# An experts' loop with branches: one region of fixed order instead of many, and the next expert's rows requested ahead of the branch

## The chip, the cores and the metric

The kernel runs on one core of one Trainium2 chip. The metric is device time in microseconds (us) for one execution; lower is better. Engines are named as the profile names them: PE is TensorE (matmul), PEld its weight loads, DVE is VectorE, ACT is ScalarE, POOL is GpSimd, SP is SyncE, which here only issues DMA transfers. A name with a q behind it (PEldq, SPq) is an engine's instruction sequencer.

## What is computed

Three layers run one after the other: clustered attention, a dense feed-forward layer with a softmax gate, and a mixture of eight experts. The change touches the third alone:

```python
logits = x @ w_gate                       # x: 1536 tokens of 512
expert_idx = np.argmax(logits, axis=1)    # one of 8 experts per token
...
h = np.maximum(np.einsum('ecd,edf->ecf', disp, w1), 0.0)   # 512 -> 1024
y = np.einsum('ecf,efd->ecd', h, w2)                       # 1024 -> 512
...
out[i] = gate_w[i] * y[expert_idx[i], pos[i]]
```

Each expert takes at most 384 tokens. How many it gets is known only when the chip has computed the gate, so the kernel branches on the counts.

## The kernel before

Attention and the dense layer are planned together by a small list scheduler (class Plan), whose emit writes all instructions in a fixed order; the gate then counts the tokens of each expert (tile cnt) and scatters the token rows, sorted by expert, to a DRAM tensor xs. From there the experts' part begins (method run of class Experts). This is its vocabulary:

- rows (L1030) asks for an expert's token rows by one transposing DMA on SP into the tile cxT; idf (L1034) asks for the tokens' numbers; ids (L1039) is the DVE cast of these to integers. xload (L1043) puts the three into a plan. The tiles come from a pool of two, so the rows of expert e+1 take the place of those of expert e-1, and the request waits until PE has finished with these.
- gemm1 (L1059) is the first product of an expert for one slice of 128 hidden units: 12 matmuls on a 16-bit high and low part of weights and rows (ah, al and the two halves of cxT). evac (L1072) clears a PSUM bank: ACT writes the high half of the hidden layer (hr, L1076), DVE the low half (L1077).
- gemm2 (L1079) is the second product: 24 matmuls of 512 columns for 128 tokens into one bank. scale (L1086) moves it to the tile yo on ACT, put (L1089) scatters yo to the output by an indirect DMA of POOL.
- A weight piece (c_weights, L970) is a DMA of 512 KB on SP (L988), then ACT makes the 16-bit high part (L991) and DVE the low part (L992). There are eight per expert. Block e asks for expert e+2's pieces 2 to 7 and expert e+3's pieces 0 and 1, into a ring of eight buffers, and block e+1 converts them; the converts wait in the list later/last for that.

The order of the work: extra(-1) handles expert 0's first 128 tokens, first its second 128 (L1196 comes between the two and stands for eight register loads of the counts, one per expert). Then, for e = 1 to 7, block(e) runs rows2 inside one of two branches, with 256 tokens if the count r is over 192, else with 192; rows2 does gemm1 for the eight slices in four banks and converts three weight pieces between. After the branch, second does 2 x 24 gemm2 matmuls, five more pieces are converted and the next eight are asked for. Behind each expert stands a second branch (L1203), taken when it has more than 256 tokens: extra(e, 2, 2) does the third 128.

What sets the order: inside a region opened by manual_schedule the instructions keep the order in which they were written. Between regions the tile framework's scheduler is free. In the kernel before, each branch's body, first and the part behind each branch are regions of their own, and the If blocks themselves and the loop around them stand outside any; so the scheduler has moved instructions and whole branches against each other. On PE, the branch of expert e+1 (L1146) now stands ahead of the branch L1203 of expert e and, from e = 1 on, ahead of part of the gemm2 matmuls of expert e.

A branch L1203 that is not taken has an else side in which each engine waits for its own last instruction and adds what the body would have added to its semaphore. Without this the counts of the semaphores would differ between the two ways.

Of the kernel before, what the change touches and what calls it, by code (L numbers as in the profile page):

```python
# [21 lines left out]
NT = B * S  # L22
DM = H * D
DF = 1024
E = 8
CAP = 384
P = 128
# [13 lines left out]
HALF = 64  # L41
# [150 lines left out]
def ring(pool, name, n, shape, dt):  # L192
    return [pool.tile(shape, dt, tag=f"{name}{i}", name=f"{name}{i}") for i in range(n)]
# [497 lines left out]
class Moe1:  # L691
# [262 lines left out]
    def run(self, order, t):  # L954
        self.t = t
        for kind, i in order:
            getattr(self, kind)(i)
# [12 lines left out]
def c_weights(tc, pools, w1, w2):  # L970
    nc = tc.nc
    W = {}

    def piece(e, i, run=lambda eng, f: f()):
        src, kh, kl, n = ((w1, "ah", "al", KC), (w2, "bh", "bl", FC))[i // 4]
        g = i % 4
        m = n // 4
        gs = slice(g * m, (g + 1) * m)
        box = []

        def load():
            if i == 0:
                W[e] = {k: pools["cw"].tile([P, c, d], F16, tag=k, name=f"{k}_{e}")
                        for k, c, d in (("ah", KC, DF), ("al", KC, DF), ("bh", FC, DM), ("bl", FC, DM))}
            late = 8 * e + i >= FIRST
            t = pools["cs2" if late else "cst"].tile([P, m, DF * DM // (n * P)], F32, tag="wst", name=f"w_{e}_{i}", bufs=LATE if late else 3)
            box.append(t)
            nc.sync.dma_start(out=t, in_=src[e, g * m * P : (g + 1) * m * P].rearrange("(c p) f -> p c f", p=P))  # L988

        run("sp", load)  # L990
        run("act", lambda: nc.scalar.activation(W[e][kh][:, gs], box[0], AF.Copy, scale=64.0))  # L991
        run("dve", lambda: nc.vector.scalar_tensor_tensor(out=W[e][kl][:, gs], in0=box[0], scalar=64.0,  # L992
                                                          in1=W[e][kh][:, gs], op0=ALU.mult, op1=ALU.subtract))

    return W, piece


def c_piece(nc, plan, piece, e, i, at, later=None):

    n = 8 * e + i  # L1000
    j = n % 3 if n < FIRST else 3 + (n - FIRST) % LATE
    cost = dict(sp=0.6, act=0.95, dve=1.14)

    def run(eng, f):
        if eng == "sp":
            plan.add(eng, cost[eng], at, f, reads=["turn"], writes=[("cst", j)], data=0.52)
        elif later is None:
            plan.add(eng, cost[eng], at + 6, f, reads=[("cst", j)], writes=[("cw", e, i)])
        else:
            later.append((f, lambda at: plan.add(eng, cost[eng], at, f, reads=[("cst", j)], writes=[("cw", e, i)])))  # L1010

    piece(e, i, run)


class Experts:
# [125 lines left out]
    def block(self, e, start, r):  # L1141
        plan = self.plan
        plan.banks = [(0.0, k) for k in self.two]
        self.hidden(e, 2)
        last, self.later = self.later, []
        with self.tc.If(r > P + HALF) as c:  # L1146
            with self.tc.manual_schedule():
                self.rows2(e, 2 * P, last[:6])
        with c.Else():
            with self.tc.manual_schedule():  # L1150
                self.rows2(e, P + HALF, last[:6])
        with self.tc.manual_schedule():
            if e + 1 < E:
                self.xload(e + 1, 0.0, [(0, CAP)], (4.0,))
            for n, (_, conv) in enumerate(last[6:]):
                conv(1.2 + 1.2 * (n // 2))
            for n, i in enumerate(range(8 * e + start, min(8 * e + start + 8, 8 * E))):
                c_piece(self.nc, plan, self.piece, i // 8, i % 8, 0.5 + 1.0 * n, self.later)
            self.second(e, 0, 2, 0.0, [], CAP)
            plan.emit()  # L1160
# [13 lines left out]
    def run(self, ctx, start, cnt, cnt0):  # L1174
        tc, nc, plan = self.tc, self.nc, self.plan
        self.xk = ctx.enter_context(tc.tile_pool(name="cx", bufs=2))
        self.pools["cs2"] = ctx.enter_context(tc.tile_pool(name="cs2", bufs=LATE))
        one = ctx.enter_context(tc.tile_pool(name="c1", bufs=1))
        self.yo = ring(one, "yo", 3, [P, DM], F32)
        self.hr = [ring(one, f"hr{i}", 2, [P, FC, 2 * P], F16) for i in range(2)]  # L1180
        for h in self.hr:
            for x in h:
                nc.vector.memset(x[:, :, P + HALF :], 0.0)
        self.bank = [plan.banks.pop(0)[1] for _ in range(2)]
        self.four, self.two = [k for _, k in plan.banks[:4]], [k for _, k in plan.banks[4:]]
        plan.MIX, plan.WIN, plan.lean, plan.marks = 0.1, 0.05, {}, ()
        r0 = nc.values_load(cnt0[0:1, 0:1], min_val=0, max_val=NT)
        self.hidden(-1, 1)
        with tc.If(r0 > P - 1) as full:
            self.extra(-1, 0, 2)  # L1190
        with full.Else():
            self.rows(-1, 0, P)
            self.idf(-1, 0, P)
            self.ids(-1, 0, P)
            self.extra(-1, 0, 2)
        regs = [nc.values_load(cnt[0:1, i : i + 1], min_val=0, max_val=NT) for i in range(E)]  # L1196
        for e in range(E):
            if e:
                self.block(e, start, regs[e])
            else:  # L1200
                with tc.manual_schedule():
                    self.first(start)
            with tc.If(regs[e] > 2 * P):  # L1203
                self.hidden(e, 1)
                self.extra(e, 2, 2)


@with_exitstack
# [153 lines left out]
```

## Time and profile before

| | us |
|---|---|
| three runs | 573.86, 576.17, 578.21; median 576.17 |
| the profiled execution | 570.86 |
| span of its trace | 569.1 (1.8 lies around it) |
| PE busy | 495.2 (87%) |
| DVE, ACT, POOL busy | 414.0, 365.0, 277.4 |
| granted TensorE clock, mean | 0.966 of full speed |

Times in the trace count from the span's start. The experts' part runs from 383 to the end. PE's busy time counts overlapping matmuls once, and a matmul's end is modelled, so the distance between the starts of two matmuls tells more than the length of one. The experts differ: the trace has 256-column matmuls for experts 2 and 3, 192 columns for 1 and 4 to 7, and one taken branch L1203, that of expert 2.

### The profile page before, as it was taken

The numbers are of one execution on the slowest core, as the hardware profiler recorded it, in microseconds if no ns is written. First come the engines' busy times: TensorE is split into PE (matmuls) and PEld (weight loads), VectorE is DVE, ScalarE is ACT, GpSimd is POOL, SyncE is SP. The second block draws the span as 40 slices with busy tenths as digits, with TensorE's granted clock in tenths as the row PEclk, the third lists the DMA queues.
The fourth block names the chain that finished last, engine by engine and source line by source line (L and its number), as shares of the span: only waits on it lengthen the run. The fifth ranks groups of instructions, "written<-read, shape, count | busy, mean of one in ns | idle before, by whom it ended". The sixth has DMA issues, their size and how long they took to land. (4 is left out here: it accounts for less than half of the span.)

```text
span 569.1 us, 13148 instructions
## 1 busy us (share of the span) xinstructions
PE 495.2 (87%) x4945; PEld 323.1 (57%) x4945; DVE 414.0 (73%) x980; ACT 365.0 (64%) x553; POOL 277.4 (49%) x292
## 2 busy tenths in 40 slices
PE   1578899889688988989989989989799999999796
PEld 1356676666465554645544444447567585677462
DVE  6699979999989799998655999981276254756310
ACT  3576778988867888978754999941256253755220
POOL 2256788999969868898762245431000201010011
PEclk9987989999979999999999999999989999999899
DMA  8898858796769799999999788974956757889400
GB/s 246 251 183 222 251 161 224 221 278 161 174 173 214 169 239 152 196 229 168 240 186 195 214 232 203 221 191 119 313 163 245 209 192 217 241 305 294 71 20 22
DMA packets 159347, 113.85 MB, mean 200 GB/s; under 512 B 126560, under 2 KB 135074, under 8 KB 159268
## 3 DMA queue, kind: packets, MB, share of 16 engines
q1 hardware_dynamic: 156660, 106.31, 75.9%
q0 software_dynamic: 2320, 6.32, 3.1%
q8 instruction: 51, 0.84, 0.6%
q14 instruction: 28, 0.23, 0.1%
q10 hardware_dynamic: 288, 0.16, 0.1%
HBM read 51.57 MB, written 17.11 MB: 121 GB/s over the span
## 5 line engine op out<-in xcount | busy, mean ns | idle before, releaser
L409 POOL TENSOR_TENSOR pr<-pf,pr 128x384 f16<-128x384 f32 x168 | 173.7, 1064 | 53.2 <-ACT pr L461 24.8
L1090 POOL DMA_INDIRECT out_dram<-yo,ids x16 | 16.0, 1000 | 154.2 <-ACT yo L1087 130.1
L1063 PE MATMUL psb<-cxT,ah 128*128 128x192 f16 (+2 forms) x288 | 69.9, 254 | 8.7 <-DMA cxT<-xs 5.2
L503 DVE TENSOR_REDUCE mm<-psb 128x1 f32<-128x384 f32 x132 | 66.9, 546 | 6.7 <-PE psb L500 6.5
L1064 PE MATMUL psb<-cxT,ah 128*128 128x192 f16 (+2 forms) x288 | 69.8, 254 | 0.0
L1065 PE MATMUL psb<-cxT,al 128*128 128x192 f16 (+2 forms) x288 | 69.8, 254 | 0.0
L537 PE MATMUL psS<-QK 96*128 96x384 f32 x132 | 62.4, 507 | 0.0
L500 PE MATMUL psb<-QK 96*128 96x384 f32 x132 | 47.9, 422 | 15.4 <-DVE mm L503 11.2
L545 ACT ACTIVATE pf<-psS 128x768 f32<-128x768 f32 x66 | 53.0, 803 | 8.4 <-PE psS L537 7.0
L545 ACT ACTIVATE pr<-psS 128x768 f16<-128x768 f32 x66 | 52.6, 803 | 7.8 <-PE psS L537 7.3
L992 DVE SCALAR_TENSOR_TENSOR bl<-w,bh 128x1024 f16<-128x1024 f32 x32 | 39.0, 1229 | 20.4 <-ACT bh L991 19.8
L536 PE MATMUL psS<-QK 128*128 128x384 f16 x132 | 46.9, 355 | 1.7 <-ACT pr L545 1.0
L558 PE MATMUL psb<-V,pr 128*128 128x65 f16 x396 | 43.5, 196 | 3.9 <-DVE mm L503 3.1
L992 DVE SCALAR_TENSOR_TENSOR al<-w,ah 128x1024 f16<-128x1024 f32 x32 | 40.5, 1279 | 7.9 <-ACT ah L991 7.8
L1076 ACT ACTIVATE hr<-psb 128x384 f16<-128x384 f32 (+1 forms) x28 | 14.6, 520 | 47.3 <-PE psb L1065 47.3
L1083 PE MATMUL psb<-bl,hr 128*128 128x512 f16 x112 | 42.5, 379 | 0.9 <-PEq L1203 0.6
L560 PE MATMUL psb<-V,pr 128*128 128x65 f16 x396 | 43.1, 194 | 0.1
L559 PE MATMUL psb<-V,pr 128*128 128x64 f16 x396 | 43.2, 197 | 0.0
L1077 DVE SCALAR_TENSOR_TENSOR hr<-psb,hr 128x384 f16<-128x384 f32 (+1 forms) x28 | 16.6, 593 | 36.3 <-ACT hr L1076 36.3
L1082 PE MATMUL psb<-bh,hr 128*128 128x512 f16 x112 | 42.4, 379 | 0.3
L1084 PE MATMUL psb<-bh,hr 128*128 128x512 f16 x112 | 42.4, 379 | 0.1
L558 PEld LDWEIGHTS <-pr 128*128 128x128 f16 x396 | 37.2, 98 | 7.4 <-issue 2.5
(202 smaller groups left out, 1576.5 us busy)
## 6 DMA issues: line engine op xcount, KB each, us to landing
w<-in_w_dram SPq DMA_DIRECT2D x64, 512.0 KB
xs<-X SPq DMA_DIRECT2D x12, 516.0 KB
QK<-hr SPq DMA_DIRECT2D x16, 384.0 KB
QK<-hl SPq DMA_DIRECT2D x32, 192.0 KB
x<-in_qkT_dram SPq DMA_DIRECT2D x7, 768.0 KB
lT<-in_w_in_dram SPq DMA_DIRECT2D x8, 512.0 KB
lT<-in_w_out_dram SPq DMA_DIRECT2D x8, 512.0 KB
v<-in_vP_dram SPq DMA_DIRECT2D x8, 384.0 KB
```

The lines of the kernel that those rows point to most:

```text
L409: nc.gpsimd.tensor_tensor(out=out[:, i], in0=a[:, i], in1=b[:, i], op=ALU.subtract)
L500: add("pe", 0.18, at(c - 10 + 0.25 * g), lambda c=c, g=g, w=w: nc.tensor.matmul(w.bank[:, :384], q1[:, c * P : (c + 1) * P], k1[:, g * 384 ...
L503: add("dve", 0.465, at(c - 9.9 + 0.25 * g), lambda c=c, g=g, w=w: nc.vector.tensor_reduce(out=m2[mm][:, c, g : g + 1], in_=w.bank[:, :384] ...
L536: nc.tensor.matmul(o, k2[:, ks], q2[:, qs], start=True, stop=False)
L537: nc.tensor.matmul(o, k1[:, ks], q1[:, qs], start=False, stop=True)
L545: add("act", 0.691, at(k + 0.5), lambda dst=dst, kb=kb: nc.scalar.activation(dst, ps[kb][:, :, :384], AF.Exp, scale=SC), reads=[kb], write ...
L558: nc.tensor.matmul(A, ph[ub][:, c, qs], v[:, j, c, 0:65], start=(c == 0), stop=False)
L559: nc.tensor.matmul(A[:, :64], ph[ub][:, c, qs], v[:, j, c, 65:129], start=False, stop=False)
L992: run("dve", lambda: nc.vector.scalar_tensor_tensor(out=W[e][kl][:, gs], in0=box[0], scalar=64.0, in1=W[e][kh][:, gs], op0=ALU.mult, op1=A ...
L1063: nc.tensor.matmul(o, w["ah"][:, c, fs], x[:, 0, c, a:b], start=(c == 0), stop=False)
L1064: nc.tensor.matmul(o, w["ah"][:, c, fs], x[:, 1, c, a:b], start=False, stop=False)
L1065: nc.tensor.matmul(o, w["al"][:, c, fs], x[:, 0, c, a:b], start=False, stop=(c == KC - 1))
```

## The change

The loop over the experts, with the register loads, stands in one manual_schedule region, the If blocks included; the regions inside the two branches are gone. So every engine gets its instructions, branches too, as the program writes them. All eight counts are loaded into registers at the top. The rows and numbers of expert e+1 are asked for ahead of the two branches of expert e, not in the plan behind them; the cast ids stays in the plan.

```diff
         last, self.later = self.later, []
+        if e + 1 < E:
+            self.X[e + 1] = self.tiles(self.xk, e + 1, CAP)
+            self.rows(e + 1, 0, CAP)
+            self.idf(e + 1, 0, CAP)
         with self.tc.If(r > P + HALF) as c:
-            with self.tc.manual_schedule():
-                self.rows2(e, 2 * P, last[:6])
+            self.rows2(e, 2 * P, last[:6])
         with c.Else():
-            with self.tc.manual_schedule():
-                self.rows2(e, P + HALF, last[:6])
+            self.rows2(e, P + HALF, last[:6])
         with self.tc.manual_schedule():
             if e + 1 < E:
-                self.xload(e + 1, 0.0, [(0, CAP)], (4.0,))
+                plan.add("dve", 0.07, 9.0, lambda: self.ids(e + 1, 0, CAP), writes=[("ids", ((e + 1) % 2, CAP))])
...
-        regs = [nc.values_load(cnt[0:1, i : i + 1], min_val=0, max_val=NT) for i in range(E)]
-        for e in range(E):
-            if e:
-                self.block(e, start, regs[e])
-            else:
-                with tc.manual_schedule():
-                    self.first(start)
-            with tc.If(regs[e] > 2 * P):
-                self.hidden(e, 1)
-                self.extra(e, 2, 2)
+        with tc.manual_schedule():
+            regs = [nc.values_load(cnt[0:1, i : i + 1], min_val=0, max_val=NT) for i in range(E)]
+            for e in range(E):
+                if e:
+                    self.block(e, start, regs[e])
+                else:
+                    with tc.manual_schedule():
+                        self.first(start)
+                with tc.If(regs[e] > 2 * P):
+                    self.hidden(e, 1)
+                    self.extra(e, 2, 2)
```

Lines after the change are two to four higher: L1146 becomes L1150, L1196 becomes L1199, L1203 becomes L1206.

Three places show how the instructions move. The first is ACT, from the end of extra(-1) to the first branch of expert 1. hh_0 and hr10 are halves of the hidden layers of experts 0 and 1, bh and ah converted weights, w_2_5 the sixth weight piece of expert 2, yo0 the output of first. Before:

```order
L1076 ACTIVATE hh_0_6056<-psb4_4710 128x512
L1076 ACTIVATE hh_0_6056<-psb6_4712 128x512
L991 ACTIVATE bh_2_5454<-w_2_5_6152 128x1024
L991 ACTIVATE bh_2_5454<-w_2_6_6166 128x1024
L1087 ACTIVATE yo0_5646<-psb0_72 128x512
L1196 TENSOR_LOAD cnt_66
L1146 COMPARE_AND_BRANCH
L1076 ACTIVATE hr10_5651<-psb4_4710 128x512
```

Now:

```order
L1199 TENSOR_LOAD cnt_66 x8
L1076 ACTIVATE hh_0_6058<-psb4_4710 128x512
L1076 ACTIVATE hh_0_6058<-psb6_4712 128x512
L1087 ACTIVATE yo0_5646<-psb0_72 128x512
L1206 COMPARE_AND_BRANCH
L1076 ACTIVATE hh_0_6216<-psb7_4713 128x512
L1076 ACTIVATE hh_0_6216<-psb2_74 128x512
L1087 ACTIVATE yo2_5648<-psb7_4713 128x512
L1206 UNCONDITIONAL_BRANCH x2
L1150 COMPARE_AND_BRANCH
L1076 ACTIVATE hr10_5651<-psb4_4710 128x512
```

The two converts of w_2_5 and w_2_6 no longer stand ahead of yo0; they come behind the branch of expert 1. All register loads stand at the top, and the branch L1206 of expert 0 precedes that of expert 1.

The second place is SP, at the requests for the last expert's rows, cxT7. Before:

```order
L1146 COMPARE_AND_BRANCH
L1146 UNCONDITIONAL_BRANCH x2
L988 DMA w_7_7_8436<-in_w2_dram 128x2x512
L1035 DMA idf6_8390<-xs_60 128x3x1
L1203 COMPARE_AND_BRANCH
L1203 UNCONDITIONAL_BRANCH x2
L1031 DMA_TRANSPOSE cxT7_8834<-xs_60 128x8x384
L1035 DMA idf7_8835<-xs_60 128x3x1
L1146 COMPARE_AND_BRANCH
```

Now:

```order
L988 DMA w_7_7_8406<-in_w2_dram 128x2x512
L1206 COMPARE_AND_BRANCH
L1206 UNCONDITIONAL_BRANCH x2
L1031 DMA_TRANSPOSE cxT7_8573<-xs_60 128x8x384
L1035 DMA idf7_8574<-xs_60 128x3x1
L1150 COMPARE_AND_BRANCH
L1150 UNCONDITIONAL_BRANCH x2
L1206 COMPARE_AND_BRANCH
L1206 UNCONDITIONAL_BRANCH x2
L1150 COMPARE_AND_BRANCH
```

The request stands behind expert 5's branch L1203/L1206 in both. Before, that one comes behind the branch of expert 6 (the first row), so cxT7 stands just ahead of the branch of expert 7. Now it stands ahead of the branch of expert 6, a whole expert earlier. The branch L1206 of one expert and L1150 of the next now follow each other with nothing between but the requests.

The third place is PE, where first begins (psb_4713 is the bank of extra(-1), psb_4710 the first bank of first). Before:

```order
L1084 MATMUL psb_4713<-bh_4726,hl_-1_5672 128x512
L1189 UNCONDITIONAL_BRANCH
L1063 LDWEIGHTS ah_4724
L1063 MATMUL psb_4710<-cxT_6047,ah_4724 128x128
L1064 LDWEIGHTS ah_4724
```

Now:

```order
L1084 MATMUL psb_4713<-bh_4726,hl_-1_5672 128x512
L1191 UNCONDITIONAL_BRANCH
L1063 LDWEIGHTS ah_4724
L1199 TENSOR_LOAD cnt x8
L1063 MATMUL psb_4710<-cxT_6049,ah_4724 128x128
L1064 LDWEIGHTS ah_4724
```

Eight register loads have come between the first weight load of first, which waits for the rows cxT0, and its first matmul. Before, each of the eight stood ahead of the branch that uses it.

## Rows read from the trace of the kernel before

**Rows 1.** Stretches: length, busy of PE, PEld, DVE, ACT, POOL, PEclk, DMA share, GB/s

```profile
405.00:412.60 7.60, 4.12 (x49) 3.97 (x48) 1.77 (x3) 2.61 (x4) 0.00 (x0) 0.92 1.04 375
412.60:418.20 5.60, 5.56 (x36) 5.29 (x36) 4.67 (x7) 4.07 (x6) 1.35 (x1) 0.50 0.22 85
...
425.10:537.40 112.30, 107.88 (x840) 73.47 (x840) 58.70 (x65) 54.66 (x71) 10.76 (x11) 1.00 0.76 230
537.40:541.00 3.60, 3.59 (x24) 3.32 (x24) 0.17 (x1) 0.00 (x0) 0.00 (x0) 0.53 0.02 5
```

**Rows 2.** Waits of PE from 394 to the end: total us, times, longest

```profile
PE psb L1063 <- DMA cxT<-xs: 5.2, 3, 3.3
PE psb L1063 <- ACT yo L1087: 3.5, 1, 3.5
PE psb L1083 <- PEq L1203: 0.6, 1, 0.6
```

**Rows 3.** Timeline of PE, branch of expert 1: start us, us, what [idle before <-releaser]

```profile
408.87 0.25 PE L1065 MATMUL psb<-cxT,al 128*128 128x192 f16 x1
412.64 0.32 PE L1063 MATMUL psb<-cxT,ah 128*128 128x192 f16 x1 [3.52 <-ACT yo L1087]
```

**Rows 4.** Timeline of ACT, the same place

```profile
409.56 1.06 ACT L991 ACTIVATE bh<-w 128x1024 f16<-128x1024 f32 x1 [8.94 <-DMA w<-in_w_dram]
411.05 1.06 ACT L991 ACTIVATE bh<-w 128x1024 f16<-128x1024 f32 x1 [0.43 <-DMA w<-in_w_dram]
412.01 0.58 ACT L1087 ACTIVATE yo<-psb 128x512 f32<-128x512 f32 x1
412.49 0.48 ACT L1076 ACTIVATE hr<-psb 128x384 f16<-128x384 f32 x1
```

**Rows 5.** Timeline of DVE: the cast ids ahead of branch 1, last evacuation of branch 4

```profile
411.79 0.16 DVE L1041 CAST ids<-idf 128x3 int32<-128x3 f32 x1
...
490.06 0.55 DVE L1077 SCALAR_TENSOR_TENSOR hr<-psb,hr 128x384 f16<-128x384 f32 x1
```

**Rows 6.** Timeline of PE: the waits for the rows of experts 2 and 7

```profile
425.11 0.27 PE L1063 MATMUL psb<-cxT,ah 128*128 128x256 f16 x1 [1.07 <-DMA cxT<-xs]
...
533.68 0.38 PE L1083 MATMUL psb<-bl,hr 128*128 128x512 f16 x1
537.41 0.24 PE L1063 MATMUL psb<-cxT,ah 128*128 128x192 f16 x1 [3.35 <-DMA cxT<-xs]
```

**Rows 7.** Timeline of SP's requests: first weight pieces, rows of experts 2 and 7

```profile
399.70 3.42 SPq L988 DMA_DIRECT2D w<-in_w_dram  x5
...
419.54 2.82 SPq L1031 DMA_TRANSPOSE cxT<-xs  x1
...
529.77 3.02 SPq L1031 DMA_TRANSPOSE cxT<-xs  x1
```

**Rows 8.** Line L1196 on PE's sequencer: ns min/median/max, first and last start us

```profile
L1196 PEldq TENSOR_LOAD <-cnt x8: 300/306/315, 401.5 to 530.0; - x8
```

**Rows 9.** Timeline of PE where first begins

```profile
393.08 0.38 PE L1083 MATMUL psb<-bl,hh_-1_5671 128*128 128x512 f16 x1
393.30 0.38 PE L1084 MATMUL psb<-bh,hl_-1_5672 128*128 128x512 f16 x1
394.46 0.22 PE L1063 MATMUL psb<-cxT,ah 128*128 128x128 f16 x1 [0.78 <-DMA cxT<-xs]
```

**Rows 10.** Lines L1146 and L1203 on PE's sequencer: ns min/median/max, first and last start

```profile
L1146 PEldq COMPARE_BRANCH  x9: 70/291/432, 401.9 to 530.4; - x9
...
L1203 PEldq COMPARE_BRANCH  x9: 78/318/3155, 417.8 to 559.8; - x9
```

**Rows 11.** Timeline of PE: an untaken branch L1203, and the end of branch 4

```profile
444.44 0.38 PE L1083 MATMUL psb<-bl,hr 128*128 128x512 f16 x1
444.97 0.38 PE L1084 MATMUL psb<-bh,hr 128*128 128x512 f16 x1
...
489.15 0.25 PE L1065 MATMUL psb<-cxT,al 128*128 128x192 f16 x1
```

## The prediction

> **What bounds the kernel now.** I read the stretches of the experts' part first, to see which engine is full there, then PE's waits, then the timelines of the engines that PE waits for. All that the change moves lies behind 393 us, so the rest of the span stays as it is. In the long stretch from 425.1 to 537.4 PE is busy 107.9 of 112.3 us at full granted clock, while DVE and ACT are busy half of it and the DMA engines 0.76 [rows 1]. So PE bounds this part, and only time in which PE stands or runs at a lower clock can be won. The list of its waits is short: 5.2 us for the expert rows cxT, 3.5 us for ACT's yo, 0.6 us for its own sequencer at L1203 [rows 2].
>
> The 3.5 us lie in the branch of expert 1. PE stops at 408.87 and goes on at 412.64, when ACT has emptied the bank of first [rows 3]. ACT did that at 412.01 only, because two weight converts stood before it, and these waited for their DMA until 409.56 and 411.05 [rows 4]. [...] The waits for cxT are 1.07 us at expert 2 and 3.35 us at expert 7, the latter again with a lower clock behind it, 0.53 over 3.6 us [rows 1, 6]; the rest, 0.78 us, stands where first begins [rows 9]. The rows of expert 7 were requested at 529.77 and used at 537.41, so a request takes up to 7.6 us [rows 6, 7].
>
> **The change, part by part.** The sum is made for the profiled execution, 570.86 us (span 569.1 and 1.8 around it). It lies 5.3 us under the median of the three runs, 576.17; I apply the same difference to the median.
>
> *The converts behind the branch: a gain of 6.3 us.* ACT now empties first's bank as soon as PE has filled it, so the idle 3.5 us in branch 1 go [rows 3]. So does the slow stretch behind it: 5.6 us at half the clock did 2.8 us of work [rows 1]. What is late next? Branch 1 converts three pieces between its evacuations, from the first of the five requests of 399.70 [rows 7]. The two that ACT waited for came fourth and fifth and were there at 409.56 and 411.05, 1.5 us apart [rows 4]; counted back, the three landed at about 405, 406.6 and 408, before ACT needs them. DVE is held by the cast ids of expert 1, now ahead of branch 1, whose numbers had come by 411.79 at the latest [rows 5]. PE doesn't feel it within the branch, which fills four different banks. Half the branch took from 405.0 to 408.87 [rows 1, 3], so it ends near 415.3 if it starts 2.5 us later (below). DVE then needs 4 x 0.55 for evacuations and about 3 x 1.2 for converts, 5.8 us from 411.8, to 417.6; the last low half is wanted 18 gemm2 matmuls of 0.22 us later [rows 9], at 419.3. Cost nothing, and at most 0.5 us if a piece is late.
>
> *The rows asked for ahead: a gain of 6.2 us.* The request now waits for the branch L1206 that precedes the current branch, not for the one that followed it. Between it and the use lie a branch and 48 gemm2 matmuls, 48 x 0.22 = 10.6 us for these alone [rows 9], against 7.6 us for a request. Both waits go, 1.1 and 3.4 us [rows 6], and with the second the slow clock, 0.47 of 3.6 us = 1.7 us [rows 1]. On SP the request passes the branch and the eight weight requests of the block. Those start later than the rows, but each waits for a buffer that DVE must free, and each is used one block on; with the DMA engines at 0.76 I count nothing.
>
> *No tail of gemm2 behind the branch: nothing.* Before, PE had matmuls of expert e left over while ACT and DVE finished evacuating the branch of e+1. Now gemm2 of the same expert follows at once. In branch 4 the last low half was done at 490.06 + 0.55 = 490.6, 1.5 us after the last matmul began at 489.15 [rows 5, 11]; it is wanted 18 matmuls = 3.9 us later. The cover holds with 2.4 us to spare.
>
> *Eight register loads on PE: a loss of 2.5 us.* They stand behind the weight load that waits for cxT, ahead of the first matmul, so what waits for cxT waits for them too. One takes 306 ns [rows 8]; 8 x 0.306 = 2.45 us. The trace shows none back to back on PE: the lower bound is one load, 0.3 us, should they overlap; the upper 8 x 0.5 = 4 us, if each held PE up as long as an untaken branch does, 0.53 us between two starts [rows 11]. On the other engines they lie in idle time. PE's idle time there grows from 0.78 [rows 9] to 3.2 us, close to the 3.35 and 3.5 us that were followed by the lower clock. That would cost 1.7 to 2.8 us; I take 0.9, about half of the smaller one, with bounds 0 and 2.8.
>
> *Branches one behind the other: a loss of 2.2 us.* At an untaken L1203 PE runs empty: 0.53 us between two starts in place of 0.22 [rows 11], 0.3 lost. That stays, six times (experts 0, 1, 3 to 6). But L1146 had matmuls queued ahead of it; L1150 now stands right behind the emptied engine. Its compare takes 291 ns in the middle, 70 to 432 [rows 10]: 6 x 0.29 = 1.7 us, bounds 0.4 and 2.6. I add 0.5 us for instructions that come late behind two jumps; before, one untaken L1203 made PE wait 0.6 us [rows 2].
>
> [...]
>
> *Sum.* 3.5 + 2.8 + 1.1 + 3.4 + 1.7 = 12.5 us won; 2.5 + 0.9 + 2.2 = 5.6 us lost; 6.9 us net, 1.2%. That makes 563.9 us for the profiled execution and 576.17 - 6.9 = 569.3 us against the median. Bounds with the same mechanism: all losses at their low ends (0.3 + 0 + 0.4) 11.8 us won, 564.4; all at their high ends (4 + 2.8 + 2.6 + 0.5) 2.6 us won, 573.6.
>
> **Rivals.**
> 1. *The jumps stall for instructions (slower).* One untaken L1203 took 3,155 ns on PE's sequencer [rows 10], and PE's waits show only 0.6 us at that line [rows 2]: queued matmuls hid it. L1150 has none queued. At six places of 3.15 us this loses 18.9 in place of 2.2 us: 12.5 - 3.4 - 18.9 = 9.8 us slower, 586 us. It decides from three stalls on (9.1 / 3.15 = 2.9). Against it: 1 of the 18 branch records of the two lines is that long, and the jump L1206 is still taken early, while matmuls are queued, which leaves time to fetch ahead. [...]
> 2. *The stall in branch 1 stays.* If the first three pieces land late, ACT holds the high halves and gemm2 waits in place of gemm1. For it: ACT is at the DMA's mercy there, 8.94 us idle [rows 4]. Against: the count back from 409.56. The 6.3 us are not won: 0.6 us faster, 575.6 us.
> 3. *The rows still come late.* SP works in order, and the request for cxT stands behind eight weight requests that wait for DVE, which in turn waits in ids for numbers and scatters. If the last of them ends after the branch of expert 6, the 5.1 us of expert 7 are not won: 1.8 us faster, 574.4 us. Against: DVE is busy 58.7 of 112.3 us [rows 1].
> 4. *The register loads overlap and the clock holds.* 2.1 + 0.9 us less lost: 9.9 us faster, 566.3 us or less.
>
> **How the numbers follow.** Forecast 0.56, rival 1 0.08, rival 2 0.08, rival 3 0.10, rival 4 0.18. A measurement of this kernel can tell about 1%, 5.8 us. The forecast stands 1.1 us beyond that line, with bounds 4 us on either side, so about three quarters of its chance are faster by over 1% (0.43) and one quarter not (0.13). With rival 4 faster is 0.61, rounded to 0.62. Rivals 2 and 3 and the rest of the forecast are within 1%: 0.30 rounded. Rival 1 is slower, 0.08. The likeliest case alone spans 564.4 to 573.6 us. The range must hold rivals 2 and 3 too, and some of the scatter of the runs (573.9 to 578.2); it leaves out rival 1 and the best ends: 563.5 to 577 us.
>
> **What would show it.** Right: PE's list of waits has no yo L1087 and no cxT over 1 us except where first begins; there the first matmul starts about 2.5 us later than 394.46 against the matmul before it; PEclk is 1.00 from there to the end, or low once, behind that gap; the distance between starts at each untaken L1206 is 0.8 us or so. The requests for cxT come about one branch earlier on SP. Wrong: L1150 with records of 3 us on PE's sequencer and equal gaps of PE (rival 1); gemm2 waiting for hr in block 1 (rival 2); a wait for cxT at expert 7 (rival 3); a gap under 2 us where first begins (rival 4).

## The result: slower by 0.7%, with the won time spent on instructions

Twenty runs of each kernel, taken in turn, gave 571.88 us before (median) and 574.32 us after. The ratio is 1.0071, 95% interval 1.0043 to 1.0099. Ratios, here and below, are taken over the fast runs alone (a run over 1.5% above the fastest of its kernel is left out), so they need not equal the ratio of the medians. So the change makes the kernel a little slower, by 2.4 us in the medians and some 4 us by the ratio, where 6.9 us less were forecast.

First a warning on reading it. The profiled execution of after took 576.50 us (span 574.7), that of before 570.86. Of these 5.6 us, 4.9 lie ahead of the experts' part, in code that the change doesn't touch: the first matmul on cxT-1 starts at 382.98 us before and at 387.92 after. Over all 19 traces of this study, with the same code up to there, it starts anywhere between 381.6 and 389.0 us, and at 382.7 and 383.5 us in two more traces of after. That is scatter. So the comparison is made on the experts' part, from that first matmul to the end of the last one:

| | experts' part, us, in each trace |
|---|---|
| before | 180.9, 185.1 |
| after | 181.3, 184.7, 180.1 |

These differ by no more than they scatter, so the traces don't show where the measured 4 us lie. What they show is what was won and what was lost.

PE's waits in the experts' part after the change, against [rows 2] (total us, times, longest):

```profile
PE psb L1063 <- issue: 7.6, 3, 4.3
PE psb L1063 <- PEq L1206: 2.2, 4, 0.7
PE psb L1064 <- issue: 2.1, 1, 2.1
```

No wait for ACT's yo and none for cxT is left. The waits that were to go are gone. In their place stand 11.9 us that PE waits for its own instructions: "issue" is idle time in which nothing that the profile shows was missing, PEq is PE's sequencer. PE's timeline has the places, against [rows 3, 6, 9, 11] (start us, us, what, idle before and its releaser):

```profile
398.24 0.38 PE L1084 MATMUL psb<-bh,hl_-1_5672 128*128 128x512 f16 x1
402.89 0.22 PE L1063 MATMUL psb<-cxT,ah 128*128 128x128 f16 x1 [4.27 <-issue]
...
415.68 0.26 PE L1063 MATMUL psb<-cxT,ah 128*128 128x192 f16 x1 [0.47 <-PEq L1206]
...
416.44 0.25 PE L1063 MATMUL psb<-cxT,ah 128*128 128x192 f16 x1
418.74 0.26 PE L1064 MATMUL psb<-cxT,ah 128*128 128x192 f16 x1 [2.06 <-issue]
...
436.85 0.28 PE L1063 MATMUL psb<-cxT,ah 128*128 128x256 f16 x1 [0.48 <-PEq L1206]
...
488.87 0.38 PE L1084 MATMUL psb<-bh,hr 128*128 128x512 f16 x1
491.39 0.26 PE L1063 MATMUL psb<-cxT,ah 128*128 128x192 f16 x1 [2.14 <-issue]
...
512.67 0.26 PE L1063 MATMUL psb<-cxT,ah 128*128 128x192 f16 x1 [1.17 <-issue]
...
531.78 0.26 PE L1063 MATMUL psb<-cxT,ah 128*128 128x192 f16 x1 [0.65 <-PEq L1206]
...
550.79 0.26 PE L1063 MATMUL psb<-cxT,ah 128*128 128x192 f16 x1 [0.56 <-PEq L1206]
```

The first pair is where first begins: 4.65 us from start to start, 1.16 before. The rest are the branches: at each untaken L1206 PE empties, meets L1150, and starts again 0.85 to 2.52 us after the start of its last matmul; and once, at 418.74, it stops inside branch 1, ten matmuls in, with its data there. The sequencer's records of the three lines say what it did meanwhile, against [rows 8, 10] (ns min/median/max, first and last start):

```profile
L1199 PEldq TENSOR_LOAD <-cnt x8: 297/308/807, 399.1 to 402.6; - x8
L1206 PEldq COMPARE_BRANCH  x9: 78/313/3061, 411.5 to 565.2; - x9
L1150 PEldq COMPARE_BRANCH  x9: 70/288/1891, 415.4 to 550.5; - x9
```

Eight loads fill 399.1 to 402.9 without a break. One compare of L1150 takes 1,891 ns; the next longest took 918 and 400. They belong to the gaps of 2.52, 1.55 and 1.03 us; the compares of the other three places took 70 to 219 ns. Instructions arrive over a DMA queue of their own (the page's DMA queues; packets, MB, share of 16 engines):

```profile
q8 instruction: 51, 0.84, 0.6%
```

0.84 MB in 51 packets is 16 KB each. The packet records put one of them at 489.02 to 489.98 us, in the gap that ends at 491.39, and one at 416.35 to 417.45, in the gap inside branch 1. PE goes on 1.4 and 1.3 us after they end. All 19 traces agree: 47 compares on PE's sequencer in the experts' part took over 500 ns, and each of them ended 1.2 to 1.5 us after the end of such a packet. So these are waits for instructions, called fetches below.

And the clock, against [rows 1]: the two slow stretches of before are gone, but two gaps of after are followed by new ones at half the clock (PEclk 0.50); the second row takes in some full clock at both ends (length, busy of PE, PEld, DVE, ACT, POOL, PEclk, DMA share, GB/s):

```profile
403.50:406.90 3.40, 3.40 (x35) 3.40 (x33) 0.00 (x0) 0.00 (x0) 0.00 (x0) 0.50 1.05 258
491.30:496.00 4.70, 4.61 (x36) 4.42 (x37) 0.56 (x1) 1.29 (x2) 0.97 (x1) 0.64 1.23 398
```

### The profile page after: what moved, and what is told of

Its sections match the earlier page's. It is cut to its first block, busy times and chain, and to the rows that moved or that the text cites. A ratio compares the mean times of both kernels' runs of the same rounds, so it can differ in the third digit from the quotient of the medians.

```text
span 574.7 us, 13145 instructions
## 1 busy us (share of the span) xinstructions
PE 494.0 (86%) x4945; PEld 322.3 (56%) x4945; DVE 412.8 (72%) x980; ACT 363.8 (63%) x553; POOL 279.7 (49%) x292
## 5 line engine op out<-in xcount | busy, mean ns | idle before, releaser
L1090 POOL DMA_INDIRECT out_dram<-yo,ids x16 | 19.6, 1222 | 151.4 <-ACT yo L1087 67.2
L1087 ACT ACTIVATE yo<-psb 128x512 f32<-128x512 f32 x17 | 10.2, 597 | 52.7 <-PE psb L1084 27.6
L500 PEld LDWEIGHTS psb<-QK 96*128 96x128 f32 x132 | 27.0, 214 | 24.5 <-DVE mm L503 18.1
```

The lines of the kernel that those rows point to most:

```text
L500: add("pe", 0.18, at(c - 10 + 0.25 * g), lambda c=c, g=g, w=w: nc.tensor.matmul(w.bank[:, :384], q1[:, c * P : (c + 1) * P], k1[:, g * 384 ...
```

## The experiments

Theory A: the eight loads at the top, and jumps that find their target's instructions not yet there, cost what the change won. The rivals: a late transfer lies behind the loads; an emptied engine costs this much at any branch; the front is slower because of the change. "Experts' part" is as above; the expectation of run 1 and the first of run 7 count it to the start of the last matmul (180.9 us for after). Ratios are to the kernel before, run in turn with each.

**1. The loads spread over the experts.**

```diff
-            regs = [nc.values_load(cnt[0:1, i : i + 1], min_val=0, max_val=NT) for i in range(E)]
+            load = lambda i: nc.values_load(cnt[0:1, i : i + 1], min_val=0, max_val=NT)
+            regs = []
...
                         self.first(start)
+                    regs.append(load(0))
+                if e + 1 < E:
+                    regs.append(load(e + 1))
                 with tc.If(regs[e] > 2 * P):
```

> The counts are loaded one or two at a time behind the matmuls of each expert, ahead of its branch L1206, no longer all eight at the top; nothing else moves. Theory A (the eight loads stand in PE's way): the 4.65 us between the last matmul of extra(-1) and the first one of first fall to about 1.2 us as before the change, and the low clock behind them goes (1.6 us): 5.1 us less in the experts' part, 175.8 us from the first cxT-1 matmul to the last matmul where the changed kernel has 180.9; time about 569 us, 0.5% under the kernel before. Rival: it is the rows of expert 0 that are late there, and the loads only lie beside that wait; then the distance stays above 3 us with cxT as its releaser and the time stays near 574. In both theories the stalls at the branches of experts 4 to 6 (2.5, 1.6, 1.0 us) stay, as the code moves by 6 instructions only.

Measured 571.99 us, ratio 0.9975 (0.9934 to 1.0016); experts' part 182.2 us. PE's timeline:

```profile
396.15 0.22 PE L1063 MATMUL psb<-cxT,ah 128*128 128x128 f16 x1 [1.29 <-DMA cxT<-xs]
...
483.79 0.34 PE L1063 MATMUL psb<-cxT,ah 128*128 128x192 f16 x1 [3.36 <-issue]
...
506.49 0.26 PE L1063 MATMUL psb<-cxT,ah 128*128 128x192 f16 x1 [2.93 <-issue]
...
529.00 0.26 PE L1063 MATMUL psb<-cxT,ah 128*128 128x192 f16 x1 [2.41 <-issue]
```

Half right. The gap at the top falls to 1.66 us, so the loads were the cause there and the late-rows rival falls. But the gaps at three branches grew, from 2.5, 1.6 and 1.0 to 3.7, 3.3 and 2.8 us, which no theory had expected, and ate the gain in this trace. The timed runs kept some of it: 0.9975 against 1.0071 for after, with the intervals apart. The same kernel a second time, to see whether that repeats:

> The kernel with the counts loaded one at a time, once more, for its trace. Its gaps ahead of experts 4, 5 and 6 were 3.7, 3.3 and 2.8 us, where the changed kernel had 2.5, 1.6 and 1.0. If the load ahead of the compare, which takes 0.4 us of its lead, caused that, they repeat within 0.5 us; if it was the state of the DMA engines in that run, they fall by 1 us or more at some of the places.

They were 4.48, 2.19 and 2.55 us, experts' part 182.4: they scatter by up to 1.1 us but stay above those in all three traces of after, at expert 5 by 0.2 us only. So the loads are suspected, and run 3 follows it up.

**2. The changed kernel again, twice.** No edit.

> The changed kernel once more, for its trace. Theory A: the time ahead of the experts' part (387.9 us in its first trace, 382.4 to 388.9 in the others, all with the same code there) is scatter, so the first cxT-1 matmul comes anywhere from 382 to 389; the gaps at the branches stand at the same four places (in branch 1, ahead of experts 4, 5, 6). Their sizes tell what is left open: if only the place in the code sets them, they repeat within 0.3 us (2.3, 2.5, 1.6, 1.0); if the fetch also depends on what the DMA engines do just then, they differ by up to 2 us. Rival: the change itself delays the front: 387 us or more again.

> The changed kernel a third time, for its trace: experts' part 181 to 185 us; the gaps in branch 1 and ahead of experts 4 and 5 are again the long ones (2.3 to 3.7, 2.5 to 2.7, 1.6 to 2.0 us), the first matmul of the experts' part between 382 and 389 us.

The second trace began the experts' part at 382.73 us and the third at 383.51: the front is scatter, the rival of a slower front falls. The gaps stood at the same places; in branch 1 2.3, 3.7, 2.7 us, ahead of expert 4 2.5, 2.7, 2.0, of expert 5 1.6, 2.0, 1.0, of 6 1.0 three times. Place repeats, size does not. The third trace's experts' part of 180.1 us and its gap of 1.0 us ahead of expert 5 lie under what was expected.

**3. Each load right behind the branch of the expert before.** As run 1, but load(e + 1) stands behind the two branches L1150 of expert e, ahead of its gemm2 matmuls.

> The changed kernel with the count of expert e+1 loaded right behind the branch of expert e, ahead of its 48 gemm2 matmuls, in place of all eight at the top; the two compares again stand 4.2 us apart on PE's sequencer as in the changed kernel (3.8 us where the load stood just ahead of the compare). Theory A (the load took its 0.4 us from the time that the fetch has between the two jumps): the gaps ahead of experts 4, 5, 6 fall back from 3.7 to 4.5, 2.2 to 3.3 and 2.6 to 2.8 us to the changed kernel's 2.5 to 2.7, 1.6 to 2.0 and 1.0; with no loss at the top the experts' part is 181.3 or 184.7 less 3.5 and 1.6, 176 to 180 us. Rival: what comes earlier at the top makes the DMA engines collide with the fetch; the gaps stay at 2.2 us or more at all three, experts' part 182 us.

Measured 569.72 us, ratio 0.9963 (0.9919 to 1.0007); experts' part 175.9 us. PE's timeline:

```profile
485.03 0.26 PE L1063 MATMUL psb<-cxT,ah 128*128 128x192 f16 x1 [2.20 <-issue]
...
504.51 0.26 PE L1063 MATMUL psb<-cxT,ah 128*128 128x192 f16 x1 [1.03 <-PEq L1209]
...
523.62 0.26 PE L1063 MATMUL psb<-cxT,ah 128*128 128x192 f16 x1 [0.65 <-PEq L1209]
```

Gaps of 2.6, 1.4 and 1.0 us, as after; and the gap at the top is 0.74. The gaps are those of Theory A. Its reason, that the load takes its time from what lies between the jump L1206, which starts a fetch, and the jump L1150, which needs it, is argued: ahead of expert 4 the packet starts 2.8 to 3.5 us after the end of L1206's compare in this trace and the three of after, and 4.3 and 5.0 us after it in the two of run 1. Why 0.4 us of lead cost up to 1.8 us of gap isn't settled. By this one trace, loads placed so take 4 to 9 us out of the changed kernel's experts' part (180.1 to 184.7 less 175.9). The timed runs agree in direction (0.9963 against 1.0071), but don't tell this kernel from that of run 1 (0.9975).

**4. Dead code that moves the rest.** 64 small matmuls in a side that is never entered:

```diff
             self.ids(-1, 0, P)
+            for _ in range(64):
+                nc.tensor.matmul(self.bank[1][:, :P], ...)
             self.extra(-1, 0, 2)
```

> 64 small matmuls (128 instructions) stand in the branch side of L1199's neighbour that is never entered, the side in which expert 0's first rows are asked for again; nothing that runs is changed, only where the later code of PE lies. Theory A (fetches, in blocks of 256 instructions): the stalls move. The distance at the branch between experts 0 and 1 grows from 0.85 to about 2.5 us and the 2.3 us inside branch 1 go; the distances ahead of experts 4 and 5 fall from 2.5 and 1.6 to about 0.9; those ahead of experts 6 and 7 grow from 1.0 and 0.9 to about 2.5. Sum about as before, time 574 +- 2 us. Rival B (an emptied engine): every distance stays where and as it was.

The blocks of 256 instructions agree with the packets in the trace of after: from the start of its first packet to that of its 28th (32.67 to 381.58 us) PE and PEld have 6,892 records, 255 to each of the 27 packets.

Measured 581.21 us, ratio 1.0152 (1.0092 to 1.0213); experts' part 185.7 us. PE's timeline:

```profile
412.10 0.34 PE L1063 MATMUL psb<-cxT,ah 128*128 128x192 f16 x1 [2.73 <-issue]
...
485.41 0.26 PE L1063 MATMUL psb<-cxT,ah 128*128 128x192 f16 x1 [0.47 <-PEq L1208]
...
505.38 0.26 PE L1063 MATMUL psb<-cxT,ah 128*128 128x192 f16 x1 [0.66 <-PEq L1208]
...
510.25 0.26 PE L1065 MATMUL psb<-cxT,al 128*128 128x192 f16 x1 [2.05 <-issue]
...
528.95 0.26 PE L1063 MATMUL psb<-cxT,ah 128*128 128x192 f16 x1 [1.24 <-issue]
...
549.63 0.26 PE L1063 MATMUL psb<-cxT,ah 128*128 128x192 f16 x1 [0.66 <-PEq L1208]
```

This decides between fetch and emptied engine. No instruction that runs was changed (both traces have 13,145), and the gaps moved: ahead of expert 1 from 0.85 to 3.10 us, the one early in branch 1 is gone, ahead of 4 from 2.52 to 0.84, of 5 from 1.55 to 1.04, of 6 from 1.03 to 1.62. Expected and missed: expert 7 (2.5 expected, 1.04 measured), the time (574 us), and three new gaps inside branches 4 to 6 (0.93, 2.30, 1.65 us) that make the sum larger; at each of these PE goes on 1.4 us after the end of a packet. So the position of the code sets where PE waits; my picture of it is good enough for the direction, not for each place.

**5. All untaken branches L1206 left out.**

```diff
-                with tc.If(regs[e] > 2 * P):
-                    self.hidden(e, 1)
-                    self.extra(e, 2, 2)
+                if e == 2:
+                    with tc.If(regs[e] > 2 * P):
+                        self.hidden(e, 1)
+                        self.extra(e, 2, 2)
```

> The changed kernel with the branch L1206 and what stands in it left out for every expert but the third (expert 2, the only one with more than 256 tokens here); so nothing that runs with these inputs is left out but the untaken branches themselves. It prices them all. Theory A: the six gaps of 0.85 to 2.52 us, the 2.3 us inside branch 1 and 1.6 us of low clock go, 181.3 - 6.4 - 2.3 - 1.6 = 171.0 us for the experts' part, time about 564 us. Rival: a branch L1150 alone, with full queues ahead of it, also waits for instructions; then some gaps of over 1 us stay there, and the experts' part stays over 175 us.

Measured 561.51 us, ratio 0.987 (0.9794 to 0.9947); experts' part 170.9 us, 171.0 expected. PE's only wait, and the branches that stay:

```profile
PE psb L1063 <- issue: 4.3, 1, 4.3
```

```profile
L1150 PEldq COMPARE_BRANCH  x9: 70/286/334, 407.3 to 532.3; - x9
```

Nothing but the loads at the top is left, and no compare takes over 334 ns: here a branch with work queued ahead of it costs PE nothing. The untaken branches cost 9 to 14 us (180.1, 181.3 and 184.7 less 170.9); the timed runs agree, 0.987 against 1.0071. That is the price of all that hangs on them: the emptied engine, the second jump right behind the first, and the code of their bodies, which is gone too (45 packets of instructions in place of 51). This run doesn't part the three.

**6. The request behind the branch again.** The rows of e+1 asked for in the plan behind the branch, all else as after:

```diff
-        if e + 1 < E:
-            ...
-            self.idf(e + 1, 0, CAP)
...
-                plan.add("dve", 0.07, 9.0, lambda: self.ids(e + 1, 0, CAP), ...)
+                self.xload(e + 1, 0.0, [(0, CAP)], (4.0,))
```

> The one region stays, but the rows of e+1 are asked for behind the branch of expert e, first in its plan, as before the change. Theory A: once branch L1206 of e-1 stands ahead of branch e, the request has 10.4 us (48 gemm2 matmuls) against the 7.6 us it needs, so no wait for cxT comes back and the time stays at 574 us within 1.5; the asking ahead by itself is worth nothing. Rival: the asking ahead is what removed the waits; then 1.1 us at expert 2 and 3.4 us at expert 7 with their low clock come back: about 580 us.

Measured 585.87 us, ratio 1.0227 (1.0157 to 1.0296); experts' part 191.6 us. My forecast fell, but not to the rival: no wait for cxT came back. PE's longest new wait, and DVE's:

```profile
PE psb L1082 <- DVE hl L1077: 4.2, 1, 4.2
```

```profile
DVE ids L1041 <- DMA idf<-xs: 55.0, 6, 11.1
```

DVE stood 55 us in the cast ids (17.0 us, 5 times, in after), which waits for numbers requested behind the rows, and PE waited for the low halves that DVE wrote afterwards. To tell the cast from the request, the cast of expert e went to the start of its own block:

> The rows of e+1 asked for behind the branch of expert e, as in the run that came out 2% slower, but with the cast ids of expert e moved to the start of its own block. That run had no wait for cxT; its DVE stood in the cast for 55 us, and PE waited for DVE's low halves hl and hr. Theory A (the late request costs only through the cast that waits for it): the waits for DVE go and the experts' part falls from 191.6 to about 181 us, the time to that of the changed kernel, 574 us. Rival (it is the place of the request, which delays the weight pieces behind it or collides with them): the experts' part stays over 187 us.

Experts' part 183.1 us, inside the spread of after, no wait for DVE, DVE's wait for numbers 1.3 us; 577.01 us, ratio 1.0173 (1.009 to 1.0256). Theory A by the trace: for the experts' part the place of the request is worth nothing by itself once L1206 of expert e-1 precedes branch e; a cast that waits for it can cost 8 us. The five timed runs lie above after's ratio (the two intervals overlap a little), and I can't say from the trace why; so the time doesn't show that the place is worth nothing.

**7. The third-tile branch behind the next expert's branch.** This puts gemm1 and gemm2 matmuls between any two jumps:

```diff
         with c.Else():
             self.rows2(e, P + HALF, last[:6])
+        self.third(e - 1, before)
+        if e + 1 < E:
+            ...
+            self.idf(e + 1, 0, CAP)
...
+    def third(self, e, r):
+        with self.tc.If(r > 2 * P):
+            self.hidden(e, 1)
+            self.extra(e, 2, 2)
```

> The branch for the third 128 tokens of expert e-1 comes behind the branch of expert e (and the request for the rows of e+1 behind both), so that gemm1 and gemm2 matmuls lie between any two jumps; the eight loads stay at the top. Theory A (the second of two jumps in a row waits for instructions to be fetched): no gap over 1 us at any branch, the stall of 2.3 us inside the branch of expert 1 gone too: 4.9 us of stalls and 1.6 us of low clock less, experts' part about 174.5 us, time about 568 us. Rival B (an emptied engine costs this much at each untaken branch wherever it stands): six gaps of 0.9 to 2.5 us again, now between the gemm1 and gemm2 matmuls, time about 574 us. The rows are asked for 10 us ahead of their use: no wait for cxT by either.

Measured 572.36 us, ratio 1.005 (1.0012 to 1.0087); experts' part 179.6 us. PE's waits, beside 4.5 us for the loads:

```profile
PE psb L1082 <- PEq L1142: 2.7, 2, 1.5
PE psb L1082 <- ACT bh L991: 2.7, 1, 2.7
```

Between the theories: two gaps over 1 us at the jump over the third tile (1.77 and 1.49 us) instead of none or six, and a new wait for a weight convert. The ratio, 1.005 against 1.0071 for after, shows no gain from parting the jumps alone. With the loads of run 1 added:

> Both edits at once: the counts loaded one at a time behind the matmuls, and the branch for the third 128 tokens of expert e-1 behind the branch of expert e. Theory A (loads in PE's way, and a second jump that waits for instructions, are separate losses): the 4.86 us ahead of first fall to 1.2 to 1.7 and the low clock behind them (1.6 us) goes, nothing else grows: the experts' part 179.6 us falls to about 174.6, time about 567.5 us, 0.9% under the kernel before. Rival: the load ahead of each compare makes the compare later, and what was won at the top comes back as longer gaps at the branches, as it did when the loads were spread alone: experts' part about 179, no gain.

> The kernel with both edits once more, for its trace. Its gaps behind the branches of experts 2, 4 and 5 were 3.4, 2.4 and 3.3 us, the same kernel with the cast moved had 1.7, 0.8 and 1.2 at the same places. If the cast's place causes the difference (through when the weight pieces are on the way), they repeat within 0.5 us; if it was scatter of single executions, they fall by 1 us or more at some of them. Experts' part 175 to 181 us.

569.35 us, ratio 0.9999 (0.9951 to 1.0047); experts' part 180.2 and 177.7 us, 174.6 expected. The gap at the top went, but the gaps behind the branches of experts 2, 4 and 5 grew to 3.4, 2.4 and 3.3 us (3.1, 2.2 and 2.5 in the second trace). The rival was nearer.

**8. And the cast in its own block.**

```diff
-            if e + 1 < E:
-                plan.add("dve", 0.07, 9.0, lambda: self.ids(e + 1, 0, CAP), ...)
+            if e > 1:
+                plan.add("dve", 0.07, 0.0, lambda: self.ids(e, 0, CAP), ...)
```

> As the one before it, and the cast ids of expert e stands first in the plan of its own block, no longer at the end of the block before. Theory A: DVE stood in this cast for 39 us in the reordered kernel (its wait for idf and for the last scatter), which made it late to free weight buffers, and so ACT's convert bh late, for which PE waited 2.7 us; with the cast moved that wait goes: experts' part about 172 us, time about 565 us. Rival: the weight pieces themselves come late, the wait for bh stays at 2 us or more and the time equals that of the kernel with both edits.

> The fastest of the general versions once more, for its trace: experts' part 169.5 us within 2, and gaps of 0.8 to 1.7 us at the three places if they are the kernel's own, up to 3.4 if they scatter.

564.58 us, ratio 0.9919 (0.9874 to 0.9964): faster than both kernels, and general (it keeps both sides of every branch, unlike run 5). Experts' part 169.5 and 171.2 us. The reason given was too small: c_both, the kernel of run 7 with the loads spread, had no wait for bh, and yet 6 to 11 us went; that the forecast of 172 us came near is luck. The same compare, behind the branch of expert 2, in that kernel and, below it, in this one:

```profile
L1142 PEldq COMPARE_BRANCH  x1: 4669/4669/4669, 433.9 to 433.9; - x1
```

```profile
L1142 PEldq COMPARE_BRANCH  x1: 2972/2972/2972, 437.6 to 437.6; - x1
```

And 2.1 us from the start of each (length, busy of PE, PEld, DVE, ACT, POOL, PEclk, DMA share, GB/s), in the same order:

```profile
433.90:436.00 2.10, 1.75 (x17) 1.32 (x14) 1.72 (x2) 1.02 (x2) 0.00 (x0) 1.00 0.69 279
```

```profile
437.60:439.70 2.10, 1.78 (x17) 1.35 (x14) 1.74 (x2) 1.02 (x2) 0.00 (x0) 1.00 0.03 8
```

The compare that falls into weight transfers (0.69) takes 4.7 us, the one with idle DMA engines (0.03) 3.0; the second traces repeat it (4.4 us at 0.66 over 1.9 us, 2.9 us at 0.08). The difference lies ahead of the packet: it starts 2.2 us after the compare in the first and 0.6 us after it in the second, and takes 1.0 and 0.9 us. The edit moves no instruction of PE. So DVE, freed of the cast, may have let the weights move in time, and the fetch seems to have waited for them. That is argued, not shown: in after one compare of L1206 took 3.1 us with the engines full (1.10). The clock gives back the rest: PEclk is 0.97 and 0.98 over the experts' part of the two traces with the cast at the block's end, 1.00 over both of these. The same move on the changed kernel alone:

> The changed kernel with one edit: the cast ids of expert e at the start of its own block. In the kernel with both edits the same move shortened the experts' part by 9 us (177.7 to 180.2 against 169.5 to 171.2), though PE waited for no cast. Theory A (DVE, no longer held, frees the weight buffers earlier; the weight transfers then end before the branches, and fetches find idle DMA engines): the gaps in branch 1 and ahead of experts 4 to 6 shrink, from 8.0 and 9.4 us in sum to 6 or less; experts' part 176 to 180 us. Rival (in this order the weight transfers are under way at the branches in any case): gaps and time as in the changed kernel, 181 to 185 us.

184.3 us, 579.99 us in four runs, ratio 1.015 (1.0092 to 1.0208): nothing won, the rival. Last, run 8 with each load behind the third tile's branch:

> The fastest general version with the load of the next count moved from just ahead of the branch to behind the branch for the third 128 tokens. Theory A: the fetch has 0.4 us more at each branch; the three gaps of 1.7, 0.8 to 1.6 and 1.2 us shrink by up to 0.4 each, experts' part 168 to 170.5 us, time within 1.5 us of that version's (564.6 us). Rival: the load now stands in the way of gemm2 behind an emptied queue, 0.4 us at each of seven experts: 172 to 174 us.

565.6 us, ratio 0.9862 (0.9806 to 0.9918), experts' part 172.1 us. The intervals of the two overlap; the trace is nearer the rival. No difference shown.

**9. The kernel before again.**

> The kernel before once more, for its trace: is its experts' part of 180.9 us typical, or was one execution of it short? Theory A (its gaps have little to do with fetches, as matmuls are queued at most of its jumps): 180.9 us within 1, one or two gaps of 3.5 us at yo and at cxT again. Rival: it scatters as much as the changed kernel's (181.3 and 184.7).

185.1 us, the rival. PE's waits:

```profile
PE psb L1063 <- DMA cxT<-xs: 5.6, 3, 3.4
PE psb L1063 <- ACT yo L1087: 4.2, 1, 4.2
PE psb L1083 <- issue: 2.5, 1, 2.5
```

The first two are those of [rows 2]; the third is a fetch, 2.92 us from start to start at 515.38, where the first trace had 1.00 us. So the kernel before had fetches that could come late too; mostly queued matmuls hid them.

## Why the prediction was wrong

The forecast was 569.3 us, 1.2% faster; it is 574.3 us, 0.7% slower. That lies inside the range and within 1% of no change, to which 0.30 was given, but on the other side of it than the forecast. That the time lies inside the range is luck in part: the forecast stood on three runs of the kernel before with a median of 576.17 us, 4.3 us above that of the twenty, and 1.0071 times that would be 580 us, outside. Step by step, in the first traces of both kernels:

- *Converts behind the branch, gain 6.3*: right. No wait for yo, no slow stretch behind it, and none of the feared waits inside branch 1 for ACT or DVE.
- *Rows asked for ahead, gain 6.2*: right in size, half right in cause. No wait for cxT is left, clock included. The prediction named the branch L1206 of the expert before, now ahead, and the earlier request together. Both kernels of run 6 show that the waits stay away with the request back behind the branch: the order of the branches, which frees the buffer in time, is enough.
- *No tail of gemm2, nothing*: right, PE waits for no hr.
- *Eight register loads on PE, a loss of 2.5 + 0.9*: mis-sized, inside its bounds: 3.5 + 1.7. The distance grew from 1.16 to 4.65 us, 3.5, because one load costs 0.41 us from start to start and one of them 0.8; and half the clock for 3.4 us cost 1.7.
- *Branches one behind the other, a loss of 2.2*: this is the step that failed. The seven gaps of after sum to 0.85 + 2.30 + 0.86 + 2.52 + 1.55 + 1.03 + 0.94 = 10.05 us, some 0.25 each being the usual distance: 8.3. Before, five gaps at L1203 came to 4 x 0.53 + 1.00 = 3.1, so 1.9. That is 6.4 us lost, and 0.36 x 4.7 = 1.7 by the clock: 8.1, where the bounds ended at 3.1. Of its terms the compares held: four of the six distances at the branches are 0.85 to 1.03 us, against the forecast's 0.53 + 0.29 = 0.82. What failed is the 0.5 us for instructions that come late. At the other two branches and inside branch 1 they cost 1.7 + 0.7 + 2.2 = 4.6 us, and the clock behind one of these gaps, which this step had at nothing, the 1.7.

Together 12.5 won and 3.5 + 1.7 + 8.1 = 13.3 lost: 0.8 us slower by this sum, 0.4 by the two traces. The rest of the measured 4 us is inside the scatter of single traces (180.1 to 184.7 against 180.9 and 185.1), so how it splits stays open.

Why did the step fail? It priced late instructions by the 0.6 us that PE had waited at an untaken L1203 [rows 2]. The maximum in [rows 10], 3,155 ns, was the better guide: that compare holds a packet too (489.48 to 490.55 us), so it was a fetch that queued matmuls hid. Rival 1 named this mechanism and got 0.08, because 1 of 18 records was long; but most of those records came from compares with work ahead of them. It had place and price wrong: 3.15 us at all six places, where two of the six had a long compare, of 1.9 and 0.9 us, since each one's packet had started 0.4 and 1.5 us ahead of it; and the third wait stood inside a branch. Rivals 2 and 3 did not happen. Rival 4 had the loads overlap; they don't (0.41 us from start to start). The packets that end 1.2 to 1.5 us ahead of each long compare's end (47 in 19 traces) agree with the wait for instructions that rival 1 named, and so does run 4, where the same code elsewhere waits elsewhere. What decides how early a packet is asked for, no run here shows.

## What to carry to other kernels

Two branches in a row, the first of which empties the engine, can lose what queued work hides at a single branch: 0.85 to 2.52 us from start to start at the untaken L1206 of after, 0.53 to 1.00 at the untaken L1203 of before. Here the untaken ones cost 9 to 14 us with their code (run 5). Putting matmuls between any two jumps was not enough by itself (run 7, 1.005); with the loads spread and the cast moved it was (run 8, 0.9919). For a compare that nothing covers, read the maximum of its records beside the median, and see whether a packet of instructions ends just ahead of its end. Register loads behind a wait stood in the engine's way one by one here, 3.5 us for the eight of after: load each value where the queue is full. That it should stand well ahead of the compare too is what the traces of runs 1 and 3 suggest; the timed runs don't show it. Before two traces are compared from end to end, compare the stretch in which they run the same code: here it differed by up to 7 us.

## What the runs showed that was not expected

- Code that never runs moved 2 us gaps from one place to another and cost 0.8% against after (1.0152 over 1.0071; the two intervals overlap a little, so the cost is not quite clear of the scatter).
- Moving one DVE cast of some 0.15 us took 6 to 11 us out of the traces of one order of the branches (4.8 us between the medians, 569.35 and 564.58) and nothing out of another. The long compares behind it were 2.9 and 3.0 us where the DMA engines stood idle, 4.4 and 4.7 where they carried weights.
- PEclk stayed at 1.00 over the whole experts' part with distances of up to 1.7 us between two starts of PE (run 8, both traces). In all 19 traces there are 37 distances of 2.5 us or more in that part. The 24 from 2.9 us up were all followed by a stretch at 0.50. Of the 13 below that five were, such as the 2.52 us at 491.39 in after, and eight weren't, such as the 2.59 us of run 3 at 485.03; two of 2.3 us were (runs 4 and 8).
